# Cosine attention feeding a gated MLP on one core: k features, one difference and one weight sum on GpSimd, the last product in two PSUM banks, and a fixed table of step priorities

## The chip, the core and the metric

The kernel runs on one core of a Trainium2 chip. The metric is the device time of one execution in microseconds (us); lower is better. Before the change the median of three runs is 285.66 us (285.08 to 286.04).

## What is computed

The inputs are `q`, `k`, `v` of shape (8 batches, 8 heads, 576 tokens, 64), `w_in` (512 x 2048) and `w_out` (2048 x 512), all float32. The output is 4608 x 512 float32.

```python
def phi(x, c, s):                       # c, s: cosine and sine of the token's place
    r = np.maximum(x, 0.0)
    return np.concatenate([r * c, r * s], axis=-1)
q_p, k_p = phi(q, cos_w, sin_w), phi(k, cos_w, sin_w)
kv  = einsum('bhsf,bhsd->bhfd', k_p, v);  z = sum(k_p, axis=2)
num = einsum('bhsf,bhfd->bhsd', q_p, kv); den = einsum('bhsf,bhf->bhs', q_p, z) + 1e-06
x = (num / den) transposed to (4608, 512)
h = x @ w_in
out = (h * cos(h)) @ w_out
```

## The kernel before

The eight batches of attention feed nine chunks of 512 tokens of the two matrix products. A batch gives 512 tokens to the chunk of its own number, and its remaining 64 tokens go into a ninth chunk (`xR`). Chunk c has a first layer (`layer1`, output `gT`) and a second (`layer2` or `layer2_plain`, output staged in one of three tiles `ost` and stored from GpSimd's queue, line L803).

**Attention of a batch.** `load` (L394, L397) fetches q, k and v by SyncE's queue into `qm`, `km`, `vm`, one tile of each for all batches, so that the load of the next batch waits until the features of this one are made. `prep` makes features: ten instructions for k and ten for q per batch (five token groups, cosine and sine), each 128x512 float32 to float16 into `KQ`, as a Relu with a scale on ScalarE (L419) or as max and multiply on VectorE (L420). `cast_v` (L433, L434) makes float16 of v. `kv` (L446) multiplies k features by v in 40 matmuls of TensorE. `q_dma` (L485) transposes the q features by a DMA of SyncE's queue, `num` (L507, then L523 to L527) gives x, and `x_dma` (L557) or `x_pe` (L547) transposes x into `xT`.

**The products.** From chunk 1 the second layer, and from chunk 3 half of the first, is a Strassen-like product of seven in place of eight block products. It needs sums and differences of the operands, made by VectorE: of the weights once (`w_out_sums` L857 makes `T1` to `T4`, `w_in_sums` L676), of x in four instructions per chunk (`layer1_sums`, L697, tiles `XS0` to `XS3`), and of `gT` (L879, L924). The gate is a sine on ScalarE (L577) and a multiplication on VectorE (L579). Results leave PSUM by ScalarE copies (L748, L908) and VectorE additions (L752, L912). In the last chunk the last product (`a22` by `T4`) adds to bank `A`, whose two halves are then copied by ScalarE (L943) and VectorE (L945) and stored by two DMAs, one from SyncE's and one from ScalarE's queue.

**The order of the work.** Nothing is issued by the functions above directly. Each calls `Plan.add` with an engine (or a choice of engines), assumed costs, a due time and the data that it reads and writes. `Plan.run` then lays all steps out with a model of the engines, and each engine gets its instructions in the order of the modelled starts. A step may have a choice of VectorE and ScalarE (`either`); the plan takes one. In the model a step with `port=True` on VectorE and one with `port=True` on GpSimd exclude each other. The plan of before starts from the due times, passes forward and backward over the steps and tries 117 random changes of the priorities, keeping the best modelled end:

```python
        now = passes([s["due"] for s in self.steps], self.PASSES)
        for _ in range(self.ROUNDS):
            amp, wide = rnd.choice((0.5, 1, 2, 4)), rnd.choice((20, 40, 80, 300))
```

GpSimd has in before only memsets, a few tiny copies that hold back loads (L970, L980, L995, L1002), the loads of the weights (L976, L990) and the stores of the output (L803).

Of the kernel before, what the change touches and what calls it, by code (L numbers as in the profile page):

```python
# [15 lines left out]


class Plan:

    LINK = {"PE": 0.12, "ACT": 0.05, "DVE": 0.05, "POOL": 0.1, "SP": 0.0}

    PASSES, ROUNDS = 12, 117  # L30

# [10 lines left out]
    def add(self, eng, occ, lat, due, fn, rd=(), wr=(), dma=None, lane=None, late=0.0,  # L42
            lazy=None, port=False):

# [26 lines left out]
    def run(self):  # L73

        best = [math.inf]
        rnd = random.Random(1)

        def passes(key, n):
            local = None
            for _ in range(n):
                start, done = self.forward(key)
                end = max(done)
                if end < best[0]:
                    best[:] = [end, start, done, [s["eng"] for s in self.steps]]
                key = self.backward(start, done, end)
                if local is None or end < local[0]:
                    local = end, key  # L90
            return local
        now = passes([s["due"] for s in self.steps], self.PASSES)
        for _ in range(self.ROUNDS):
            amp, wide = rnd.choice((0.5, 1, 2, 4)), rnd.choice((20, 40, 80, 300))
            mid = rnd.uniform(0, best[0])
            key = [k + (rnd.gauss(0, amp) if abs(k - mid) < wide / 2 else 0) for k in now[1]]
            new = passes(key, 4)
            if new[0] < now[0] + 0.02:
                now = new
        for s, a, b, e in zip(self.steps, *best[1:]):  # L100
            s["start"], s["end"] = a, b
            s.update(zip(("eng", "occ", "lat", "fn"), s["opts"][e]))
        return sorted(self.steps, key=lambda s: (s["start"], s["n"]))

# [112 lines left out]

    def backward(self, start, done, end):
        st = self.steps
        left = [0] * len(st)  # L220
        for s in st:
            for d in s["deps"]:
                left[d] += 1
            if s["prev"] is not None:
                left[s["prev"]] += 1
        limit = [end - done[n] + start[n] for n in range(len(st))]
        late = [0.0] * len(st)
        free = {e: end for e in self.LINK}
        ready = {e: [] for e in self.LINK}
        for n, k in enumerate(left):  # L230
            if not k:
                ready[st[n]["eng"]].append(n)
        for _ in st:
            best = None
            for e, cand in ready.items():
                if not cand:
                    continue
                at = {n: min(free[e], limit[n] + st[n]["occ"]) for n in cand}
                top = max(at.values()) - self.PATIENCE.get(e, 0.0)
                k, t, n = max((start[n], at[n], n) for n in cand if at[n] >= top)  # L240
                if best is None or t > best[0]:
                    best = (t, e, n)
            t, e, n = best
            ready[e].remove(n)
            late[n] = free[e] = t - st[n]["occ"]
            for d in st[n]["deps"]:
                limit[d] = min(limit[d], late[n] - self.link(d, n) - (done[d] - start[d]))
                left[d] -= 1
                if not left[d]:
                    ready[st[d]["eng"]].append(d)  # L250
            d = st[n]["prev"]
            if d is not None:
                limit[d] = min(limit[d], late[n] - 0.01)
                left[d] -= 1
                if not left[d]:
                    ready[st[d]["eng"]].append(d)
        return late


@with_exitstack  # L260
def kernel(
# [24 lines left out]
    def blocks(ap, n):  # L286
        return ap.rearrange("(p f) ... -> f p ...", f=2)[n]
# [66 lines left out]
    Q_PE, X_PE = (), range(1, 3)  # L354
    VCAST = ("DVE", "ACT")
    LAZY = 8.0
    LATE_BY, LATE_W = (0.0, 1.0, 3.0, 1.0), 0.6
# [19 lines left out]
    def either(due, cost, fn, rd, wr):  # L377

        lat = {"DVE": 0.13, "ACT": 0.15, "POOL": 0.15}
        pl.add([(e, cost[e], cost[e] + lat[e], fn[e]) for e in cost], 0, 0, due, None, rd, wr, port=True)  # L380

# [28 lines left out]
    def prep(b, nm, t, g, eng, due, hs=slice(0, H), after=()):  # L410
        dst = (kp if nm == "k" else qp)
        out_, in_ = dst[:, t, hs, g, :], raw[nm][:, hs, t, :]
        sc = CS[:, b % 2, g, t:t + 1]
        heads = range(H)[hs]
        rd = hk(nm, heads) + ["CS", *after]
        wr = [(nm + "p", t, g, h) for h in heads]
        f = len(heads) / H
        cost = {"DVE": 0.09 + 0.33 * f, "ACT": 0.12 + 0.5 * f}
        fn = {"ACT": lambda: nc.scalar.activation(out=out_, in_=in_, func=AF.Relu, scale=sc),  # L419
              "DVE": lambda: nc.vector.tensor_scalar(  # L420
                  out=out_, in0=in_, scalar1=0.0, scalar2=sc, op0=ALU.max, op1=ALU.mult)}
        either(due, {e: c for e, c in cost.items() if eng in (e, "")}, fn, rd, wr)

# [265 lines left out]
    def layer1_sums(c, X, xk):  # L689
# [6 lines left out]
        def tt(n, a, b, rd, wr=()):  # L696
            dve(0.33, start[c] - 1 + 0.3 * n, lambda: nc.vector.tensor_tensor(  # L697
                out=XS[n], in0=a, in1=b, op=ALU.subtract), xk + rd, [("XS", i, n)] + list(wr), port=True)
        tt(0, b12, b11, [], (hk("k") + hk("q") + hk("v") + ["AL"]) if c == B - 1 else
# [105 lines left out]
    def store(c, h, o, due, fs=None):  # L805
        O = ost[o]
        keys = [("ost", o, f) for f in range(2)]
        if c < B:
            n = c % 2
            five, four = rows(c)  # L810
            put(due, five[:, 2 * h:2 * h + 2, :], blocks(O, n), keys, nc.gpsimd, "POOL")
            put(due, four[:, 2 * h:2 * h + 2, :], blocks(O, 1 - n), keys, nc.gpsimd, "POOL")
            return
        for n in range(2):
            f = slice(0, Dm) if fs is None else slice(fs * MH, (fs + 1) * MH)
            dst = out.rearrange("(i n s) m -> n i s m", n=2, s=S)[n][2 * h:2 * h + 2, 0:S5, f]
            put(due, dst.rearrange("i (p t) m -> p t i m", t=NT + 1)[:, NT], blocks(O, n)[:, :, f],
                keys if fs is None else [("ost", o, fs)],
                *((nc.scalar, "ACT") if n else (nc.sync, "SP")), nb=262.0 if fs is None else 131.0)

# [29 lines left out]
    def w_out_sums():  # L850
# [4 lines left out]

        def tt(out_, a, b, op, rd, wr):
            dve(1.14, start[2] - 8, lambda: nc.vector.tensor_tensor(  # L857
                out=out_, in0=a, in1=b, op=op), rd, wr, port=True)
        tt(T3, b22, b12, ALU.subtract, wk, ["T3"])
        tt(T1, b12, b11, ALU.subtract, wk, ["T1"] + wk[0:2])  # L860
# [3 lines left out]
    def layer2(c):  # L864
# [24 lines left out]

        def product(bank, a, b, rd, first, last):  # L890
            n = next(order)
            for tt in range(2):
                due = w0 + (n - 0.5 + 0.5 * tt) / 7 * ww * 0.97

                def mm(tt=tt):
                    for j in range(JH):
                        nc.tensor.matmul(  # L897
                            bank[0][:, tt * MH:(tt + 1) * MH], lhsT=a[:, j, tt * P:(tt + 1) * P],
                            rhs=b[:, j, :], start=(first and tt == 0 and j == 0),
                            stop=(last and tt == 1 and j == JH - 1), skip_group_check=True)  # L900
                pe(JH, MMH, due, mm, rd, [bank[1]])
            return due
# [33 lines left out]
        if c == B:  # L936
            store(c, 1, oh, d + 1.0, 1)
        d = product(A, a22, T4, gk(1, 1) + ["T4"], False, True)
        if c < B:
            copy(ost[oh][:, :, m0], A, [("ost", oh, 0)], d + 0.5)  # L940
            store(c, 1, oh, d + 1.5)
        else:
            act(0.3, d, lambda: nc.scalar.activation(  # L943
                out=ost[oh][:, 0, m0], in_=view(A)[:, 0], func=AF.Copy), [A[1]], [("ost", oh, 0)])
            dve(0.33, d, lambda: nc.vector.tensor_copy(  # L945
                out=ost[oh][:, 1, m0], in_=view(A)[:, 1]), [A[1]], [("ost", oh, 0)])
            store(c, 1, oh, d + 1.0, 0)


# [111 lines left out]
    def attention(b):  # L1061
# [3 lines left out]
        for t in range(NT + 1):  # L1065
            for g in range(2):
                prep(b, "k", t, g, "", T + 1.2 * t)
        for t, nt in ((0, 2), (2, 2), (4, 1)):
            cast_v(b, t, "", T + 6 + 0.4 * t, nt=nt)
        kv(b, T + 8)  # L1070
        for t in range(NT + 1):
            due = T + 8 + 1.2 * t
            for g in range(2):
                prep(b, "q", t, g, "", due)
            if b in Q_PE:
# [68 lines left out]
```

## Time and profile before

| | |
|---|---|
| median of 3 runs | 285.66 us (285.08 to 286.04) |
| profiled execution, span from first to last instruction | 282.8 us |
| the median less this span | 2.9 us; a device time of the profiled execution itself is not listed |
| TensorE busy, share of the span | 272.4 us, 96% |
| VectorE busy | 247.5 us, 88% |
| ScalarE busy | 215.5 us, 76% |
| GpSimd busy | 26.0 us, 9% |
| granted TensorE clock | 0.998 |
| k features: ScalarE L419, 56 of 128x512 | 38.3 us, 719 ns each |
| k features: VectorE L420, 24 of 128x512 | 10.7 us, 489 ns each |

A busy TensorE in this table is not TensorE at its peak, since ends of matmuls are modelled. VectorE and ScalarE instructions overlap by some 0.1 us at their ends, so that the busy time of a group is less than its count times its mean. "Idle before, releaser" in a group tells how long the engine stood idle just before such an instruction and what ended the wait.

### The profile page before, as it was taken

How to read it: one execution, taken by the hardware profiler on the slowest of the kernel's cores; microseconds unless marked ns; L12 is line 12 of the kernel's file. 1: busy time of each engine (PE TensorE's matmuls, PEld its weight loads, DVE VectorE, ACT ScalarE, POOL GpSimd, SP SyncE). 2: the span in 40 equal slices, each digit the busy share in tenths (PEclk: the TensorE clock that was granted, in tenths of full speed). 3: DMA queues.
4: the chain of work that ended last, by engine and by line, in shares of the span. 5: the costliest groups of instructions: out<-in, count | busy, mean ns of one | idle time of the engine just before them, and what ended most of it. 6: DMA issues, size and time to landing. Idle time of an engine off the chain costs nothing.

```text
span 282.8 us, 6578 instructions
## 1 busy us (share of the span) xinstructions
PE 272.4 (96%) x2619; PEld 208.3 (74%) x2619; DVE 247.5 (88%) x458; ACT 215.5 (76%) x367; POOL 26.0 (9%) x53
## 2 busy tenths in 40 slices
PE   7889989999999999999999999999999999999993
PEld 2468856669866688777877887787777877876882
DVE  2986878999999999999999999999899999967941
ACT  2947897999999999999999999995834666456420
POOL 1412020011000020002000200020002001100200
PEclk9999999999999999999999999999999999999999
DMA  6999999799989999999997899786024001100124
GB/s 214 303 204 273 258 310 300 251 270 212 344 222 240 228 227 362 170 245 224 254 268 186 265 290 224 164 159 167 2 56 168 21 2 75 76 2 0 68 82 150
DMA packets 77567, 53.30 MB, mean 188 GB/s; under 512 B 46048, under 2 KB 75232, under 8 KB 77536
## 3 DMA queue, kind: packets, MB, share of 16 engines
q1 hardware_dynamic: 70032, 39.73, 55.7%
q0 software_dynamic: 6784, 12.59, 17.1%
q10 hardware_dynamic: 720, 0.57, 0.6%
q8 instruction: 20, 0.33, 0.5%
q14 instruction: 11, 0.09, 0.1%
HBM read 36.74 MB, written 9.44 MB: 163 GB/s over the span
## 4 chain that ended last, share of the span: by engine, by line
PE 84%; DMA 8%; ACT 3%; DVE 2%; issue 1%; SPq 0%; ACTq 0%; DVEq 0%
PE M L897 33%; PE M L636 16%; PE M L740 8%; PE M L604 8%; PE TR L740 4%; PE M L834 4%; DMA vm<-in_v_dram 4%; PE TR L636 3%; PE ATT L507 3%; DMA qT<-KQ 3%; PE ATT L446 3%; DMA qm<-in_q_dram 2%; ACT KQ L419 1%; PE M L475 1%; DVE x L527 1%
## 5 line engine op out<-in xcount | busy, mean ns | idle before, releaser
L577 ACT ACTIVATE ch<-M 128x512 f32<-128x512 f32 x90 | 52.8, 595 | 11.1 <-PE M L604 4.1
L897 PEld LDWEIGHTS <-gT 128*128 128x128 f16 x560 | 53.7, 98 | 9.3
L579 DVE TENSOR_TENSOR gT<-M,ch 128x512 f16<-128x512 f32 x83 | 55.4, 683 | 4.7 <-ACT ch L577 4.2
L897 PE MATMUL M<-w_out_sb,gT 128*128 128x256 f16 x448 | 54.9, 273 | 0.0
L636 PE MATMUL M<-xT,w_in_sb 128*128 128x512 f16 x184 | 45.9, 379 | 0.0
L419 ACT ACTIVATE KQ<-qm,CS 128x512 f16<-128x512 f32 x59 | 40.1, 718 | 4.5 <-DMA qm<-in_q_dram 4.5
L419 ACT ACTIVATE KQ<-km,CS 128x512 f16<-128x512 f32 x56 | 38.3, 719 | 0.0
L636 PEld LDWEIGHTS <-w_in_sb 128*128 128x128 f16 x256 | 24.4, 98 | 18.3
L803 POOL DMA_DIRECT2D out_dram<-ost x32 | 17.0, 537 | 213.9 <-DVE ost L912 134.8
L897 PE MATMUL M<-T,S 128*128 128x256 f16 x256 | 32.5, 273 | 0.0
L604 PE MATMUL M<-xT,w_in_sb 128*128 128x256 f16 x256 | 30.6, 273 | 0.1
L897 PEld LDWEIGHTS <-S 128*128 128x128 f16 x256 | 24.9, 98 | 4.0
L604 PEld LDWEIGHTS <-w_in_sb 128*128 128x128 f16 x256 | 24.5, 98 | 3.9 <-issue 0.3
L908 ACT ACTIVATE ost<-M 128x512 f32<-128x512 f32 x31 | 18.5, 597 | 10.2 <-PE M L897 10.1
L527 DVE TENSOR_TENSOR x<-ATT,rec 128x512 f16<-128x512 f32 x32 | 22.1, 691 | 1.1
L740 PEld LDWEIGHTS <-w_in_sb 128*128 128x128 f16 x192 | 18.5, 98 | 4.9 <-issue 0.2
L912 DVE TENSOR_TENSOR ost<-M,ost 128x512 f32<-128x512 f32 x24 | 16.4, 681 | 4.0 <-issue 3.5
L507 PEld LDWEIGHTS <-qT 128*128 128x128 f16 x320 | 15.1, 98 | 4.7 <-issue 0.5
L752 DVE TENSOR_TENSOR Z<-M,Z 128x512 f32<-128x512 f32 x23 | 15.6, 684 | 2.3 <-PE M L740 1.9
L879 DVE TENSOR_TENSOR S<-gT 128x2048 f16<-128x2048 f16 (+1 forms) x16 | 17.3, 1085 | 0.2
L748 ACT ACTIVATE Z<-M 128x512 f32<-128x512 f32 x19 | 11.3, 596 | 6.6 <-PE M L740 6.4
L740 PEld LDWEIGHTS <-WS 128*128 128x128 f16 x144 | 13.6, 98 | 3.3 <-issue 0.2
(130 smaller groups left out, 421.8 us busy)
## 6 DMA issues: line engine op xcount, KB each, us to landing
out_dram<-ost POOLq DMA_DIRECT2D x32, 256.0 KB, 4.3
qm<-in_q_dram SPq DMA_DIRECT2D x8, 640.0 KB, 5.8
km<-in_k_dram SPq DMA_DIRECT2D x8, 640.0 KB, 7.8
qm<-in_q_dram SPq DMA_DIRECT2D x8, 512.0 KB, 5.6
km<-in_k_dram SPq DMA_DIRECT2D x8, 512.0 KB, 6.7
vm<-in_v_dram SPq DMA_DIRECT2D x6, 640.0 KB, 6.4
vm<-in_v_dram SPq DMA_DIRECT2D x6, 512.0 KB, 5.9
w_in_sb<-in_moe_w_in_dram POOLq DMA_DIRECT2D x4, 512.0 KB, 8.9
```

Source lines behind the costliest of these rows:

```text
L419: fn = {"ACT": lambda: nc.scalar.activation(out=out_, in_=in_, func=AF.Relu, scale=sc), "DVE": lambda: nc.vector.tensor_scalar(out=out_, i ...
L507: nc.tensor.matmul(bank[hb][:, hh * D1:(hh + 1) * D1], lhsT=a[:, h, :], rhs=z[:, h, :], start=(i == 0), stop=(i == len(parts) - 1))
L527: nc.vector.tensor_tensor(out=split(x16[n][:, hs, :], k), in0=A[:, :, :, 0:D], in1=split(rec[n][:, hs], k).unsqueeze(3).broadcast_to((P, k ...
L577: act(0.5, due, lambda: nc.scalar.activation(out=ch[c], in_=bank, func=AF.Sin, bias=math.pi / 2.0, scale=1.0), [key], [("ch", c)])
L579: mul(due, 0.61, lambda q: q.tensor_tensor(out=dst, in0=bank if len(dst.shape) == 2 else bank.rearrange("p (j s) -> p j s", j=dst.shape[1] ...
L604: nc.tensor.matmul(M1[m][:, jj * 2 * P:(jj + 1) * 2 * P], lhsT=w_in_sb[:, cc, j * P:(j + 1) * P], rhs=X[:, cc, ts], start=(cc == 0), stop= ...
L636: nc.tensor.matmul(M, lhsT=w_in_sb[:, cc, j * P:(j + 1) * P], rhs=X[:, cc, :], start=(cc == 0), stop=(cc == NCT - 1))
L740: nc.tensor.matmul(bank[0][:, j * TH:(j + 1) * TH], lhsT=a(cc, j), rhs=b[:, cc, :], start=(first and j == 0 and cc == 0), stop=(last and j ...
L803: pl.add(eng, 0.9 if eng == "POOL" else 0.65, 0, due, lambda: q.dma_start(out=dst, in_=src_), keys, [], dma=(nb, 355.0))
L879: dve(0.07 + 1.07 / NG, due, lambda: nc.vector.tensor_tensor(out=out_[:, sl], in0=a[:, sl], in1=b[:, sl], op=op), rd, wr, port=True)
L897: nc.tensor.matmul(bank[0][:, tt * MH:(tt + 1) * MH], lhsT=a[:, j, tt * P:(tt + 1) * P], rhs=b[:, j, :], start=(first and tt == 0 and j == 0),
L908: act(0.5, due, lambda: nc.scalar.activation(out=dst, in_=view(bank), func=AF.Copy), [bank[1]], dk)
```

## The change

From batch 2 on all ten k feature instructions of a batch have GpSimd as their only engine (60 instructions). `XS2`, one of the four differences of x, goes from VectorE to GpSimd in each of the six chunks that have it. The weight sum `T3` goes from VectorE to GpSimd. The last product of the last chunk no longer adds to bank `A`: bank `A` is copied to `ost` while that product runs into two other banks, one for each half; VectorE adds each half to `ost`, and each half is stored by two DMAs of half the size. The random search is gone: a table of 1319 numbers, one for each step in the order of `add`, gives the priorities, and the plan is one forward pass with them. GpSimd's steps do not have `port=True`.

The diff, cut to its core:

```diff
+KEYS = (
+    -85, 45, 175, 387, -79, -14, 51, 116, 181, 246, 311, 376, 1113, 1267, 1502, 1163, 1972, 2582,
...
+)
     def run(self):
-        best = [math.inf]
-        rnd = random.Random(1)
...
+        st = self.steps
+        assert len(KEYS) == len(st)
+        start, done = self.forward([k / 100 for k in KEYS])
+        for s, a, b in zip(st, start, done):
             s["start"], s["end"] = a, b
...
+    XPOOL = (2,)
+    KPOOL, QPOOL = (0, 1), ()
...
     def prep(b, nm, t, g, eng, due, hs=slice(0, H), after=()):
-        cost = {"DVE": 0.09 + 0.33 * f, "ACT": 0.12 + 0.5 * f}
+        cost = {"DVE": 0.09 + 0.33 * f, "ACT": 0.12 + 0.5 * f, "POOL": 0.15 + 0.75 * f}
+              "POOL": lambda: nc.gpsimd.tensor_scalar(
+                  out=out_, in0=in_, scalar1=0.0, scalar2=sc, op0=ALU.max, op1=ALU.mult),
...
     def layer1_sums(c, X, xk):
+            if n in XPOOL:
+                pl.add("POOL", 1.3, 1.45, due - 2, lambda: nc.gpsimd.tensor_tensor(
+                    out=XS[n], in0=a, in1=b, op=ALU.subtract), rd, wr)
...
     def w_out_sums():
+            if pool:
+                pl.add("POOL", 4.7, 4.9, start[2] - 8, lambda: nc.gpsimd.tensor_tensor(
+                    out=out_, in0=a, in1=b, op=op), rd, wr)
-        tt(T3, b22, b12, ALU.subtract, wk, ["T3"])
+        tt(T3, b22, b12, ALU.subtract, wk, ["T3"], True)
...
+    def store_tile(o, i, due):
+        for n in range(2):
+            dst = out.rearrange("(i n s) m -> n i s m", n=2, s=S)[n][2 + i, 0:S5, 0:MH]
+            put(due, dst.rearrange("(p t) m -> p t m", t=NT + 1)[:, NT], blocks(ost[o], n)[:, i, 0:MH],
+                [("ost", o, 0, i)], *((nc.scalar, "ACT") if n else (nc.sync, "SP")), nb=65.5)
...
     def layer2(c):
-            act(0.3, d, lambda: nc.scalar.activation(
-                out=ost[oh][:, 0, m0], in_=view(A)[:, 0], func=AF.Copy), [A[1]], [("ost", oh, 0)])
-            dve(0.33, d, lambda: nc.vector.tensor_copy(
-                out=ost[oh][:, 1, m0], in_=view(A)[:, 1]), [A[1]], [("ost", oh, 0)])
-            store(c, 1, oh, d + 1.0, 0)
+        copy(ost[oh][:, :, m0], A, [("ost", oh, 0, i) for i in range(2)], d + 0.5)
+        d = product(BANKS2, a22, T4, gk(1, 1) + ["T4"], True, True, True)
+        for i, (bank, key) in enumerate(BANKS2):
+            dst = ost[oh][:, i, m0]
+            dve(0.33, d, lambda dst=dst, bank=bank, i=i: nc.vector.tensor_tensor(
+                out=dst, in0=bank[:, i * MH:(i + 1) * MH], in1=dst, op=ALU.add), [key, ("ost", oh, 0, i)],
+                [("ost", oh, 0, i)])
+            store_tile(oh, i, d + 1.0)
...
     def attention(b):
-                prep(b, "k", t, g, "", T + 1.2 * t)
+                prep(b, "k", t, g, "POOL" if g in KPOOL else "", T + 1.2 * t)
```

In the built program GpSimd has 60 feature instructions, 6 differences and `T3` more, and one more instruction ahead of its first feature, which loads a library of GpSimd's. The features of batch 2 and `T3` stand between the loads of `w_out` and the stores of chunk 0. The features that stay with a choice are split anew: q features on VectorE are 24 in place of 21, on ScalarE 56 in place of 59; k features of the first two batches are 11 on VectorE and 9 on ScalarE. TensorE has as many instructions of each kind as before, in another order, with few differences in the first 40 us.

## The prediction

> **What bounds the kernel now.** I read the share of the engines first, then the busy time by stage, then what TensorE waits for, then the end.
>
> The page's engine line says nothing yet of a bound:
>
> ```profile
> PE 272.4 (96%) x2619; PEld 208.3 (74%) x2619; DVE 247.5 (88%) x458; ACT 215.5 (76%) x367; POOL 26.0 (9%) x53
> ```
>
> By stage (span, then PE, PEld, DVE, ACT, POOL busy us, clock, DMA share, GB/s), all three engines are nearly full from 60 to 200 us, and after that TensorE and VectorE:
>
> ```profile
> 60.00:200.00 140.00, 139.76 (x1428) 109.26 (x1426) 134.60 (x239) 131.49 (x224) 9.52 (x18) 1.00 0.95 233
> 200.00:278.00 78.00, 77.93 (x657) 60.94 (x654) 65.42 (x109) 39.29 (x67) 6.34 (x12) 1.00 0.16 53
> ```
>
> TensorE stands still for 0.24 and 0.07 us there. Busy ends are modelled, so I check the starts: in the chain of waits eight 128x256 matmuls follow each other in 0.87 us (109 ns each), four 128x512 in 0.86 (216 ns). Its waits are few, and asked for 60 to 278 us alone the same view lists none:
>
> ```profile
> PE M L475 <- ACT KQ L419: 1.6, 1, 1.6
> PE ATT L965 <- POOL S L951: 1.3, 1, 1.3
> PE M L834 <- DMA w_out_sb<-in_moe_w_out_dram: 0.7, 1, 0.7
> PE ATT L507 <- DVE kvz L460: 0.4, 1, 0.4
> PE TR L547 <- DVE x L527: 0.3, 1, 0.3
> PE M L475 <- DVE qT L481: 0.2, 1, 0.2
> PE ATT L446 <- ACT V L433: 0.2, 1, 0.2
> ```
>
> So TensorE is the bound, at full clock, and the other two just keep up with it. The change takes no matmul away. It can gain only what is idle: these waits and the end. It can lose much more.
>
> **The feature work that leaves.** Start to start, a feature costs 0.396 us on VectorE and 0.613 on ScalarE (the rows' 0.48 and 0.72 overlap the next one), a difference 0.335, `T3` 1.13. Off VectorE go 13 k features (5.1), six differences (2.0) and `T3` (1.1), and three q features come (1.2): 7.0 us less. Off ScalarE go 47 k and three q features: 50 x 0.613 = 30.7 us less. For the time this is worth 0: TensorE waits for neither from 60 us on. It is slack, 0.31 us of idle time at most turned into gain; I take 0.2.
>
> **What GpSimd pays.** No row shows an elementwise GpSimd instruction of full size. Nearest is its memset of 128x512 float16, 0.524 us, which only writes. A feature that reads while it writes costs at least that, 0.52; one pass after the other 1.05. I take 0.9, near the upper end, since its input is twice as wide and it does two operations. `T3` is four times as long with two inputs: between 2.1 (four memsets) and 6.3 (three passes); I take the middle, 4.2. A difference is 0.52 to 1.57, middle 1.05. The Trainium skill, "GPSIMD Engine Reference", section "Elementwise — side-by-side cycle accounting", speaks against the whole move (elementwise work is slower there than on VectorE) and gives 769 ns for 512 elements in its best loop and 4497 ns for a two-input 2048; by these the chain below would be 12.2 us in place of 13.2.
>
> Per batch that is 10 x 0.9 + 1.05 + four store issues of 0.54 = 12.2 us of some 26.5: no throughput bound. The place that counts is batch 2. In the built order GpSimd makes two features, `T3`, then eight features, and only then the kv matmuls of batch 2 may run. The k load lands at 37.43 + 12.3 = 49.7 us (issue and longest time to landing in the view of tile km), the last `w_out` piece at 36.70 + 12.7 = 49.4. GpSimd is then free: in before it did nothing from 37.5 to 57.55, which also covers the library load ahead of the first feature (unseen in the trace, 0 to 12 us without cost). 49.7 + 10 x 0.9 + 4.2 = 62.9. TensorE reaches these 40 matmuls at about 64.4: in before the second half starts at 64.05, and by the counts of matmuls ahead the new order has 0.3 us more in front. Cover 1.5 us; bounds 57.0 (7.4 early) and 66.5 (2.1 late).
>
> **The shared port.** Now the waits that are new. GpSimd beside VectorE features looks like this (start, us, engine):
>
> ```profile
> 23.76 0.19 POOL L980 COPY w_out_sb<-w_in_sb 1x4 f16<-1x4 f16 x1 [6.16 <-DMA w_in_sb<-in_moe_w_in_dram]
> 35.14 0.53 POOL L1002 CAST w_out_sb<-qm 1x2 f16<-1x2 f32 x1 [9.24 <-DMA qm<-in_q_dram]
> 34.35 1.27 DVE L420 TENSOR_SCALAR KQ<-km,CS 128x512 f16<-128x512 f32 x3
> ```
>
> Two copies of a few elements: 0.19 us alone, 0.53 when VectorE's features run until 35.62. So 0.34 us per GpSimd instruction that meets them. In return L420 took 611 ns at most, where the median is 478: 0.13 us. From 49.7 to 64.4 VectorE has, in the new order, five q features, two casts of v, `T1` and `T2`: 5 x 0.396 + 0.34 + 0.60 + 2 x 1.13 = 5.2 us, 35% of the stretch. 11 instructions x 0.34 x 0.35 = 1.3: the chain ends at 64.2, 0.2 before TensorE asks. That costs 0, barely.
>
> The Trainium skill, "SBUF — State Buffer", section "Who interferes with whom", says that the later of the two waits until the first has finished, also where VectorE only reads two SBUF inputs. The copy above agrees; for two-input instructions no row here shows it. Taken whole, the rule would add all of VectorE's 5.2 us to GpSimd's chain and end it 3.7 us late.
>
> **Moved steps and their queues.** The stores of chunk 0 now stand behind batch 2's features on GpSimd (57.55 before, 62.9 or later now); chunk 1's second tile of results needs `ost0` only in its second layer, which starts at 68.6 and writes it late: 0. Chunk 1's stores stand behind batches 3 and 4; chunk 1 stored at 101.93 before, and batch 4's features end about ten us after batch 3's kv, which has 77.3 us of matmuls ahead of it and so stands near 87, with the 10 us of idle time until then: 0. SyncE's k load of batch 3 must wait for GpSimd (62.9, in before 55.95), but the order now has the four q transposes ahead of it; landing in 5.3 us and ten features give 77 to 78 against a kv at 87, cover 9 us. `T3` is read near 90 by the same count. `XS2` is read by the fifth product of its group, four products of 0.43 later, cover 1.7 against 1.05; uncovered it costs 0.7 a chunk.
>
> **The start.** Of the seven waits the first two (first load, memset) stay. The other five, 1.8 us, may move with the order: two qT copies now stand behind the casts of v, which wait for their load, and the second `w_out` load is issued behind a 0.18 us copy. Bounds +0.9 and -1.8; I take -0.3, near nothing, since the loads are the same.
>
> **The end.** Before:
>
> ```profile
> 277.96 0.38 ACT L943 ACTIVATE ost<-M 128x256 f32<-128x256 f32 x1 [4.77 <-PE M L897]
> 278.38 0.42 DVE L945 COPY ost<-M 128x256 f32<-128x256 f32 x1 [1.60 <-ACT ost L943]
> 278.84 0.64 ACTq L803 DMA_DIRECT2D out_dram<-ost  x1
> ```
>
> One bank, so the two copies follow each other. In two banks half 0 is added under half 1's matmuls, and half 1's addition (0.42, as the 128x256 additions from PSUM) ends 0.45 after the last matmul in place of 0.88: 0.43 less. Against it: three DMA issues of 0.64 or more now follow each other on ScalarE's queue, and the last may start as late as before. For it: the last DMAs are half as long. Bounds 0 and -0.8; I take -0.5.
>
> **Sum.** -0.2 - 0.3 - 0.5 = -1.0. On the profiled span that is 282.8 to 281.8; the median of the runs lies 2.9 above that span, so 285.66 becomes 284.7. The forecast's own range is 283.4 to 286.0.
>
> **Rivals.** First, GpSimd is late for batch 2's kv (slower). Place: 64.4 us, TensorE in order with nothing to put ahead. It decides as soon as a feature with its waits costs over about 1.05 us (14.7 us to land, less 4.2, over ten). At 1.05 and 6.3 plus 1.3 of waits the chain ends at 67.8, 3.4 late; with VectorE's 5.2 us shut out it is 3.7 late. TensorE never makes that up: +3.5 - 1.0 gives 288.2. For it: the copy of 0.53 us and a cover of 0.2. Against it: the memset's 0.52 leaves room.
>
> Second, VectorE becomes the bound between 60 and 200 us: it has 5.4 us free there and wins 7. Some 80 of its instructions there use the port; if each waits half a feature (0.45) in the 37% of the time in which GpSimd works, that is 13.3 of these 12.4. Whole features would give 26.6, so 0 to +14, taken as +4; less 1.0 that is 288.7. Against it: the 0.13 of the row, 80 x 0.13 = 10.
>
> Third, more is gained: all 1.8 us of the start's waits and the end's 0.43: 283.1. For it, freer engines at 40 to 60 us; against it, loads that do not move.
>
> **Chances.** The forecast 0.55, late GpSimd 0.25, VectorE the bound 0.08, the larger gain 0.12. A measurement here tells 0.3%, 0.86 us. The forecast's sum lies on that edge: 0.30 faster, 0.25 same. With 0.12 from the larger gain and 0.01 from a small lateness: faster 0.42, same 0.26, slower 0.32. The range 283.0 to 289.0 takes in the late cases and most of the larger gain.
>
> **What would show it.** Right: no wait of TensorE from 60 to 278 us; features of 0.8 to 1.0 us on GpSimd; kv of batch 2 waiting for no one near 64; the last store issued 0.4 us after the last addition's old place or earlier. Wrong: a wait of TensorE's L446 for GpSimd's `KQ`; VectorE features or gate sums much over 0.48 and 0.68 us; a TensorE busy share under 99% in the middle.

## The result and the profile after

| | before | after |
|---|---|---|
| median | 285.65 us (4 runs) | 344.25 us (339.51 to 346.32, 4 runs) |
| profiled execution: span, time | 282.8 us, not listed | 337.4 us, 339.51 us |
| granted clock of it | 0.998 | 0.939 |

The kernel became much slower: the ratio is 1.195, with a 95% interval of 1.190 to 1.200. Two of the four runs were slower at a lower clock still and are left out of the ratio; the other two have a median of 341.4 us, 55.8 us above before, and the losses and gains below are counted from there. The prediction was 284.7 us in a range of 283.0 to 289.0.

The page of the changed kernel, its engine line and GpSimd's first group:

```profile
PE 284.4 (84%) x2619; PEld 215.4 (64%) x2619; DVE 253.2 (75%) x442; ACT 188.5 (56%) x317; POOL 164.9 (49%) x120
...
L444 POOL TENSOR_SCALAR KQ<-km,CS 128x512 f16<-128x512 f32 x60 | 126.3, 2118 | 34.3 <-DMA km<-in_k_dram 19.8
```

A feature took 2118 ns on GpSimd, where the prediction had taken 900. TensorE's share fell from 96% to 84%. The span is 54.6 us longer. Of these TensorE was idle for 42.6 (337.4 - 284.4 = 53.0, before 282.8 - 272.4 = 10.4) and busy for 12.0 more with the same 2619 matmuls. By stage (span, then PE, PEld, DVE, ACT, POOL busy us, clock, DMA share, GB/s), the changed kernel:

```profile
60.00:200.00 140.00, 113.34 (x1071) 86.20 (x1069) 108.70 (x181) 82.21 (x138) 96.74 (x58) 0.93 0.82 190
200.00:278.00 78.00, 61.48 (x572) 48.10 (x570) 53.71 (x89) 36.80 (x63) 42.59 (x30) 0.87 0.42 108
```

These are the two stretches of time in which TensorE stood still for 0.24 and 0.07 us before (the work in them is not quite the same, since the changed kernel is behind). Now no engine is full: TensorE has 81%, VectorE 78%, GpSimd 69% from 60 to 200 us. That is the picture of engines that wait for each other in turn, not of an engine that is the bound. The view of waits names them for TensorE (us in total, times, longest):

```profile
PE ATT L472 <- POOL KQ L444: 25.3, 7, 8.2
PE M L772 <- POOL XS L726: 12.7, 2, 10.2
PE M L630 <- DVE gT L605: 3.7, 2, 2.4
```

The first is the one that the prediction gave as the sign of its first rival (then L446, now L472). The first two sum to 38.0 us, beside the 42.6 us of idle time that came in. GpSimd's timeline over batch 2 shows the chain that the prediction had summed (start, us, count at the end of the name), and over batch 6 where `XS2` stands:

```profile
49.88 3.98 POOL L444 TENSOR_SCALAR KQ<-km,CS 128x512 f16<-128x512 f32 x2 [12.84 <-DMA km<-in_k_dram]
53.84 4.05 POOL L898 TENSOR_TENSOR T<-w_out_sb 128x2048 f16<-128x2048 f16 x1
57.89 16.68 POOL L444 TENSOR_SCALAR KQ<-km,CS 128x512 f16<-128x512 f32 x8
...
190.52 19.94 POOL L444 TENSOR_SCALAR KQ<-km,CS 128x512 f16<-128x512 f32 x9
210.43 1.15 POOL L726 TENSOR_TENSOR XS<-xT 128x512 f16<-128x512 f16 x1
```

TensorE's timeline at the ends of these two chains (the wait and its releaser in brackets):

```profile
74.63 2.33 PE L472 MATMUL ATT<-V,KQ 128*128 128x65 f16 x39 [7.16 <-POOL KQ L444]
...
211.62 1.01 PE L772 MATMUL M<-XS,WS 128*128 128x256 f16 x4 [10.16 <-POOL XS L726]
```

The features of batch 2 begin at 49.88, where the prediction had 49.7, and end at 74.57, where it had 62.9 to 64.2. TensorE had nothing else to do from 67.47 on, 7.16 us before its next matmul. At 210.43 the 1.15 us of `XS2` come after nine features: TensorE's product waited 10.16 us for it.

The last two additions and stores of the changed kernel, which answer to the copies and the store shown of before:

```profile
332.94 0.82 DVE L993 TENSOR_TENSOR ost<-M,ost 128x256 f32<-128x256 f32 x2 [0.66 <-ACT ost L954]
333.39 1.42 ACTq L835 DMA_DIRECT2D out_dram<-ost  x2
```

The last matmul ends at 333.29 and the span at 337.36, 4.07 us later; before these were 277.93 and 282.78, 4.85 us. So the end gained 0.8 us.

### The profile page after: what moved, and what is told of

Read it like the earlier page. It is cut to its first block, busy times and chain, and to the rows that moved or that the text cites. A ratio compares the mean times of both kernels' runs of the same rounds, so it can differ in the third digit from the quotient of the medians.

```text
span 337.4 us, 6606 instructions
## 1 busy us (share of the span) xinstructions
PE 284.4 (84%) x2619; PEld 215.4 (64%) x2619; DVE 253.2 (75%) x442; ACT 188.5 (56%) x317; POOL 164.9 (49%) x120
## 3 DMA queue, kind: packets, MB, share of 16 engines
q1 hardware_dynamic: 70048, 39.73, 48.2%
## 5 line engine op out<-in xcount | busy, mean ns | idle before, releaser
L444 POOL TENSOR_SCALAR KQ<-km,CS 128x512 f16<-128x512 f32 x60 | 126.3, 2118 | 34.3 <-DMA km<-in_k_dram 19.8
L835 POOL DMA_DIRECT2D out_dram<-ost x32 | 17.9, 562 | 84.9 <-DVE ost L958 52.7
L662 PE MATMUL M<-xT,w_in_sb 128*128 128x512 f16 x184 | 47.3, 391 | 0.0
L443 ACT ACTIVATE KQ<-qm,CS 128x512 f16<-128x512 f32 x56 | 37.7, 713 | 4.3 <-DMA qm<-in_q_dram 4.3
L662 PEld LDWEIGHTS <-w_in_sb 128*128 128x128 f16 x256 | 25.1, 100 | 20.7 <-issue 2.0
L472 PE MATMUL ATT<-V,KQ 128*128 128x65 f16 x280 | 15.1, 220 | 25.3 <-POOL KQ L444 25.3
L630 PE MATMUL M<-xT,w_in_sb 128*128 128x256 f16 x256 | 31.8, 278 | 4.3 <-DVE gT L605 3.7
L943 PE MATMUL M<-T,S 128*128 128x256 f16 x256 | 33.5, 277 | 0.0
L472 PEld LDWEIGHTS <-KQ 128*128 128x128 f16 x320 | 15.1, 114 | 28.5 <-POOL KQ L444 26.2
L630 PEld LDWEIGHTS <-w_in_sb 128*128 128x128 f16 x256 | 25.0, 100 | 8.7 <-issue 4.9
L489 ACT ACTIVATE kvz<-ATT 128x520 f16<-128x520 f32 x7 | 4.2, 605 | 33.5 <-PE ATT L472 33.4
L772 PEld LDWEIGHTS <-w_in_sb 128*128 128x128 f16 x192 | 18.7, 100 | 5.7 <-issue 1.1
```

The costliest lines, as they stand in the source:

```text
L444: "POOL": lambda: nc.gpsimd.tensor_scalar(out=out_, in0=in_, scalar1=0.0, scalar2=sc, op0=ALU.max, op1=ALU.mult),
L472: nc.tensor.matmul(bank[hb][:, hh * D1:(hh + 1) * D1], lhsT=kp[:, t, h].rearrange("p g d -> p (g d)"), rhs=V1[:, t, h, :], start=(t == 0), ...
L630: nc.tensor.matmul(M1[m][:, jj * 2 * P:(jj + 1) * 2 * P], lhsT=w_in_sb[:, cc, j * P:(j + 1) * P], rhs=X[:, cc, ts], start=(cc == 0), stop= ...
L662: nc.tensor.matmul(M, lhsT=w_in_sb[:, cc, j * P:(j + 1) * P], rhs=X[:, cc, :], start=(cc == 0), stop=(cc == NCT - 1))
L772: nc.tensor.matmul(bank[0][:, j * TH:(j + 1) * TH], lhsT=a(cc, j), rhs=b[:, cc, :], start=(first and j == 0 and cc == 0), stop=(last and j ...
L835: pl.add(eng, 0.9 if eng == "POOL" else 0.65, 0, due, lambda: q.dma_start(out=dst, in_=src_), keys, [], dma=(nb, 355.0))
```

## The experiments

The theory after the result was that the price of a feature on GpSimd is the step that failed. The rivals were the port that VectorE and GpSimd share, and the order that the table of priorities fixes.

**The features go back.** `XS2`, `T3`, the table and the new end stay.

```diff
-    KPOOL, QPOOL = (0, 1), ()
+    KPOOL, QPOOL = (), ()
```

> The k features of batches 2 to 7 go back to the plan's choice of VectorE and ScalarE; XS2, T3, the table of priorities and the new end stay. Theory (a GpSimd feature costs 1.98 us by itself where 0.9 was assumed, and ten of them in series hold up kv): nearly the whole loss goes, 284 to 289 us. Rival 1 (the shared port is what costs, and T3 and XS2 on GpSimd hold VectorE too: T3 held one q feature for 3.0 us): 288 to 295. Rival 2 (the order from the table is bad by itself): over 300.

Measured: 293.26 us, ratio 1.027 (1.024 to 1.030). Of the 55.8 us lost, 48.2 come back with the features. But 7.7 stay, more than the theory had: the time lies in the range of the port rival. That rival cannot be the whole cause, since most of the loss is gone; what the 7.7 us are is asked by the next run and three later ones.

**The features alone.** `XS2` and `T3` go back to VectorE, the features stay on GpSimd.

```diff
-    XPOOL = (2,)
+    XPOOL = ()
-        tt(T3, b22, b12, ALU.subtract, wk, ["T3"], True)
+        tt(T3, b22, b12, ALU.subtract, wk, ["T3"])
```

> Only the k features stay on GpSimd; XS2 and T3 return to VectorE. Theory: the loss stays but for T3's 4.05 us in the chain of batch 2 and two waits for XS2 (12.7 us in the list of waits): 325 to 340 us. Rival 1 (port): more returns, since T3 blocked VectorE longest: 310 to 325. Rival 2 (table): no change, 339 to 345.

Measured: 341.39 us, ratio 1.197 (1.189 to 1.204), as the whole change. The theory's 325 to 340 was missed, and the time lies where the table rival had it; but the table with the new end alone takes 287.55 us (below), so the table is not what makes the loss. The 12.7 us of waiting for `XS2` are gone, and the waits for `KQ` are 36.8 us in place of 25.3: the lateness is that of GpSimd's queue, and whoever asks next pays it. So the two losses that the view of waits lists apart do not add up to two gains.

**The price by itself.** A kernel that computes nothing of the reference, with GpSimd instructions one after the other.

```python
g.tensor_scalar(out=o(i), in0=in_, scalar1=0.0, scalar2=sc[:, 0:1], op0=ALU.max, op1=ALU.mult)  # as the kernel
g.tensor_scalar(out=o(i), in0=in_, scalar1=0.0, scalar2=None, op0=ALU.max)                      # one operation
g.tensor_copy(out=o(i), in_=in_)                                                               # a cast
```

> Computes nothing of the reference: GpSimd instructions by themselves, six of each form with VectorE at rest, then eight features beside VectorE features, beside two-input VectorE differences, and beside VectorE products from PSUM. Theory: the feature as the kernel has it costs 1.98 us with VectorE at rest, and what costs is the second operation or the scalar read per partition: one operation alone 0.8 to 1.2, a cast 0.5 to 0.8; strides, float32 and the output's type change it by under 0.2; about 0.1 us are fixed, so 128x256 costs 1.0. Beside VectorE features or two-input instructions it is 0.1 to 1.2 longer, beside products from PSUM not. Rival 1 (port): under 1.0 at rest and 2.0 only beside VectorE.

Its groups (busy us, mean ns of one), in order: the kernel's form, one operation, 256 columns, the difference's form, 128 columns, the cast:

```profile
L56 POOL TENSOR_SCALAR kq<-km,sc 128x512 f16<-128x512 f32 x6 | 11.9, 1998 | 9.1 <-DMA km<-in_k_dram 9.1
...
L60 POOL TENSOR_SCALAR kq<-km 128x512 f16<-128x512 f32 x6 | 8.8, 1503 | 0.0
L71 POOL TENSOR_SCALAR kq<-km,sc 128x256 f16<-128x256 f32 x6 | 6.8, 1205 | 0.0
L73 POOL TENSOR_TENSOR o<-flat 128x512 f16<-128x512 f16 x6 | 6.1, 1108 | 0.0
L71 POOL TENSOR_SCALAR kq<-km,sc 128x128 f16<-128x128 f32 x6 | 4.2, 773 | 0.0
L62 POOL CAST kq<-km 128x512 f16<-128x512 f32 x6 | 3.4, 637 | 0.0
```

Start to start the feature takes 1.973 us with VectorE at rest, one operation 1.450, the cast 0.552; 256 columns take 1.120 and 128 take 0.693. Without strides, with a float32 output and with a float16 input it is the same within 0.003 us. So what is dear in this form of instruction is its arithmetic: the first operation adds 0.90 us to the cast (the expectation had 0.8 to 1.2 for the whole instruction), the second 0.52, or 0.43 with both scalars as constants (1.885 us). The number of operations alone does not give the price, though: the difference, one operation on two float16 inputs, takes 0.998. Then eight features ran beside VectorE instructions: features as GpSimd's, differences of 2048 columns with two inputs in SBUF, and products with one input in PSUM (start, us for all eight):

```profile
100.78 17.51 POOL L80 TENSOR_SCALAR kq<-km,sc 128x512 f16<-128x512 f32 x8
...
119.76 23.24 POOL L80 TENSOR_SCALAR kq<-km,sc 128x512 f16<-128x512 f32 x8
...
143.54 15.81 POOL L80 TENSOR_SCALAR kq<-km,sc 128x512 f16<-128x512 f32 x8
```

Beside the products a feature costs what it costs alone (15.81 / 8 = 1.98). Beside VectorE's features it is 2.19 on average, with VectorE done after half of the stretch. Beside the differences it is 2.9, and the differences take 1.26 and 1.63 us in turn, where in before such an instruction takes 1.13 start to start. The port is real, but in the kernel it adds only some 0.12 us to a feature (mean 2.118 against 1.998 here); the price makes 1.10 of the 1.22 us by which the prediction was short.

**Half as wide.** Each GpSimd feature computes heads 0 to 3 alone.

```diff
-                  out=out_, in0=in_, scalar1=0.0, scalar2=sc, op0=ALU.max, op1=ALU.mult),
+                  out=out_[:, 0:HB], in0=in_[:, 0:HB], scalar1=0.0, scalar2=sc, op0=ALU.max, op1=ALU.mult),
```

> As the changed kernel, but each GpSimd feature covers heads 0 to 3 alone (128x256); the k features of heads 4 to 7 of batches 2 to 7 are left out. Number, order and queues of the instructions stay. Theory: a feature costs about 1.0 us, the prediction's 0.9 within 0.1, and then the rest of the prediction should hold: 284 to 290 us, kv of batch 2 waiting under 2 us. Rival 1 (port): there are as many meetings with VectorE, so at least half of the loss stays: 300 to 315. Rival 2 (table): over 320.

Measured: 299.47 us, ratio 1.045 (1.039 to 1.052); 1306 ns a feature in the kernel, waits for `KQ` 1.6 us. The theory's 284 to 290 was missed, with its price of 1.0 (1.12 by itself); that at least half of the loss stays, as the port rival had it, is false as well, since a quarter stays. The chain of batch 2 ended at 67.36, and TensorE had stood waiting from 66.24. By the prediction's rule, which turns at 1.05 us a feature, this had to be late, and it is by 1.2 us. The rest of the 14 us was not traced; `XS2` makes 3.6 us of TensorE's waits.

**Half as many.** Only the sine features of k go to GpSimd, at full width.

```diff
-    KPOOL, QPOOL = (0, 1), ()
+    KPOOL, QPOOL = (1,), ()
```

> The change as it is, but only five of the ten k features of a batch (the sine ones) on GpSimd; the other five are back on ScalarE and VectorE. GpSimd then has 5 x 2.1 + 1.2 + 2.2 = 13.9 us of the 26.5 of a batch, about what the prediction had reckoned for ten at 0.9 (12.2). Theory: the lateness goes nearly whole, since per batch there is room, and the time is that of the features-back run plus little: 291 to 300, with waits for KQ under 6 us in all. Rival (the late start and the port decide, not the sum per batch): 305 to 325.

Measured: 299.12 us, ratio 1.046 (1.040 to 1.052), waits for `KQ` 3.2 us. Half the work in either way gives the same time, with 30 instructions here and 60 there. That fits GpSimd's total (66.5 us busy with features here, 77.6 there) and not the number of instructions that meet on the port. It does not show it, since the two runs differ in VectorE's and ScalarE's work too: here the other five features are made there, in the half-width run half of each is made nowhere.

**A quarter as wide.** As half as wide, with heads 0 and 1 alone.

```diff
-                  out=out_, in0=in_, scalar1=0.0, scalar2=sc, op0=ALU.max, op1=ALU.mult),
+                  out=out_[:, 0:HB // 2], in0=in_[:, 0:HB // 2], scalar1=0.0, scalar2=sc, op0=ALU.max, op1=ALU.mult),
```

> The change as it is, but every GpSimd feature computes only heads 0 and 1 of its eight (128 columns instead of 512; heads 2 to 7 of the k features are left out from batch 2 on). By itself such an instruction takes 0.69 us, below the 0.9 that the prediction took. Full width (1.98) gave 344, half width (1.12) 299.5. Theory A, the price was the failed term and the rest of the sum holds: with 0.69 TensorE waits nowhere for KQ, and what stays over the table alone (287.55) is T3's and XS2's hold on VectorE: 289 to 294. Rival B, the number of meetings on the port counts and not the price: 60 instructions more make 295 to 300. Rival C, the prediction as it stood: 283.4 to 286.0.

Measured: 286.77 us, ratio 1.005 (1.003 to 1.007). This run is the prediction's own case, since a feature now costs in the kernel what the prediction took. Its group, and GpSimd's and TensorE's timelines at batch 2:

```profile
L444 POOL TENSOR_SCALAR KQ<-km,CS 128x128 f16<-128x128 f32 x60 | 52.6, 888 | 43.0 <-DMA km<-in_k_dram 22.2
...
51.09 4.07 POOL L898 TENSOR_TENSOR T<-w_out_sb 128x2048 f16<-128x2048 f16 x1
55.15 7.58 POOL L444 TENSOR_SCALAR KQ<-km,CS 128x128 f16<-128x128 f32 x8
...
65.36 0.83 PE L472 MATMUL ATT<-V,KQ 128*128 128x65 f16 x22
```

888 ns with the port's waits, the chain done at 62.73 (predicted 62.9 to 64.2), kv of batch 2 at 65.36 (predicted 64.4), and no wait of TensorE for GpSimd's `KQ` in the whole run. The time lies inside the prediction's range and 2.1 us over its forecast. It lies in none of the three ranges on record before the run: under theory A, which added the hold of `T3` and `XS2` to the table's time, and over the prediction's own. Every instruction keeps its place, and only the width of GpSimd's features, and so their price, differs: 341.4 became 286.77 us, 54.6 of the 55.8.

**What is left: the table, `T3`, `XS2`.** Three runs without any feature on GpSimd: neither `T3` nor `XS2` there, `T3` alone, `XS2` alone (the edits of the first two experiments, combined).

> GpSimd gets no elementwise work at all: the features, XS2 and T3 are back on ScalarE and VectorE; what is left of the change is the table of priorities and the last product in two banks. It settles where the 7.7 us come from that stayed when only the features went back (293.3 us against 285.5). Theory A, the port: T3 and XS2 on GpSimd held two-input VectorE instructions (VectorE was lengthened by 8.2 us in that run), so without them the time is 284 to 286.5, and no VectorE instruction over 3 us is left. Theory B, the table: its priorities were made for another division of the work, so that the order itself costs the 7.7 us; then 290 to 294, with the same waits of TensorE for gT, S and Z. Both in halves: 287 to 290.

> Table and new end as in the change; of the work on GpSimd T3 alone stays (one instruction of 4.05 us), features and XS2 are back. With neither T3 nor XS2 there the time was 287.55 us, with both 293.3. Theory A, the early hold: T3 holds a VectorE feature of batch 2 for 3.3 us at 50 us, and in an order that is fixed nothing makes it up, so 289.5 to 291.5. Rival B, the hold is hidden, since VectorE has slack there: 287 to 288.5, and XS2 is the costly one.

> Table and new end; of the work on GpSimd the six XS2 stay (1.2 us each), features and T3 are back. Theory A: XS2's six meetings with two-input VectorE instructions lengthened those by 4.2 us in the run with both, in the stage where TensorE and VectorE are both full, so about half of the 5.7 us between that run and the table alone is theirs: 289.5 to 291.5. Rival B: XS2 itself is fast and early enough, and T3 carries the loss: 287 to 288.5.

Measured: 287.55 us, ratio 1.007 (1.004 to 1.009), with neither; 289.61, 1.015 (1.012 to 1.017), with `T3`; 289.89, 1.015 (1.013 to 1.017), with `XS2`; and 293.26 with both. So the table's order with the new end costs 1.7 us, `T3` 2.1 more, the six `XS2` 2.3, and both together somewhat more than their sum. The first lies where both theories in halves had it (287 to 290), the other two where theory A had them. What `T3` and `XS2` do to VectorE is seen in the timelines. In the run with `T3` alone:

```profile
50.41 3.73 DVE L446 TENSOR_SCALAR KQ<-km,CS 128x512 f16<-128x512 f32 x2
...
49.40 4.06 POOL L898 TENSOR_TENSOR T<-w_out_sb 128x2048 f16<-128x2048 f16 x1 [12.53 <-DMA w_out_sb<-in_moe_w_out_dram]
```

Two VectorE features that take 0.48 us each last 3.73: the first started inside `T3` and ended 0.28 us after it. In the run with `XS2` alone a gate product with two inputs in SBUF (median 1.22 us) is lengthened beside a difference:

```profile
232.23 2.10 DVE L801 TENSOR_TENSOR gT<-Z,ch 128x1024 f16<-128x1024 f32 x1
...
231.91 1.35 POOL L726 TENSOR_TENSOR XS<-xR 128x512 f16<-128x512 f16 x1 [10.92 <-DMA xR<-x]
```

VectorE's instructions over their medians (counting those over by 0.1 us and more) sum to 3.5 us in the first run and 3.7 in the second, 7.5 in the run with both and 0.7 in the run with neither. In none of these runs is a wait of TensorE for GpSimd's `XS2` listed. So the hold on VectorE is the likely cause; by which wait it comes to TensorE was not followed.

**The end alone.** The kernel before, with its search, and the last product in two banks with four smaller stores.

```diff
-        d = product(A, a22, T4, gk(1, 1) + ["T4"], False, True)
+        copy(ost[oh][:, :, m0], A, [("ost", oh, 0, i) for i in range(2)], d + 0.5)
+        d = product(BANKS2, a22, T4, gk(1, 1) + ["T4"], True, True, True)
```

> The kernel before with one part of the change: the last product in two banks and its results stored in four half-size DMAs. Search, features, differences and T3 are as before. Theory (the step on the end in the prediction): 0.3 to 0.8 us less, that is 284.7 to 285.3 if before gives 285.5; the last store is issued 0.4 to 0.8 us sooner after the last matmul. Rival: the search draws another order for the rest, since it has other steps, and the middle moves by more than the end, up or down by 1 us.

Measured: 285.34 us against 285.84, ratio 0.999 (0.996 to 1.002). From the last matmul to the end it is 4.18 us (279.42 to 283.60) where before had 4.85, so the 0.7 us are there in the trace; the comparison of times cannot tell them from nothing. The rival has a part in it: the search drew another order, and the last matmul of this trace ends 1.5 us later than in before (277.93).

**Could a better order carry the change?** The random search of before lays out the changed kernel, with measured costs of GpSimd's steps: as it is, then with that order kept and the features a quarter as wide, then with a plan that also excludes GpSimd's steps from VectorE's marked ones. And with `T3` and `XS2` on GpSimd but no features. The second pair of lines is the third run's against the first; the difference and `T3` get `port=True` there too.

```diff
-        cost = {"DVE": 0.09 + 0.33 * f, "ACT": 0.12 + 0.5 * f, "POOL": 0.15 + 0.75 * f}
+        cost = {"DVE": 0.09 + 0.33 * f, "ACT": 0.12 + 0.5 * f, "POOL": 0.15 + 1.85 * f}
...
-    pl.add([(e, cost[e], cost[e] + lat[e], fn[e]) for e in cost], 0, 0, due, None, rd, wr, port="POOL" not in cost)
+    pl.add([(e, cost[e], cost[e] + lat[e], fn[e]) for e in cost], 0, 0, due, None, rd, wr, port=True)
```

> All of the change on GpSimd stays, but the order is planned anew by the random search of before, with the measured prices of GpSimd's instructions (2.0 us a feature where the change assumes 0.9, 1.15 a difference, 4.05 for T3). It asks whether the order or the division of work is at fault. Theory A, division: ten features, a difference and four store issues are 10 x 2.1 + 1.2 + 2.2 = 24.4 us of the 26.5 us of a batch, so a plan that knows it can hide most of it but not the start of the GpSimd chain and not the port: 295 to 320, the waits for KQ down to under 20 us in all. Rival B, wrong order: with true prices the plan hides everything, 286 to 290. Rival C: nothing helps, 335 to 345.

> The order planned for the measured prices (the run of 322.2 us), with the GpSimd features computing heads 0 and 1 alone, 0.69 us each (heads 2 to 7 of the k features are left out from batch 2 on). No instruction changes its place on its engine. Theory A, the division of work: the 36 us that this order loses at full width are GpSimd's price and what VectorE's two-input instructions lose beside it, so the time falls to 286 to 292. Rival B, the order itself: kv and the second layers stand in poor places because the plan waited for GpSimd, and the time stays at 300 or more.

> As the run of 322.2 us, planned with the measured prices, and now the plan also counts that GpSimd's elementwise steps and VectorE's marked ones exclude each other, which the change does not count. Theory A, the division: 60 x 2.0 us of GpSimd and some 90 us of marked VectorE instructions want the same port in the 185 us from 50 to 235, so whoever waits, the time stays well over 300: 305 to 325. Rival B, a plan that knows the port finds the room: 287 to 297.

> T3 and XS2 on GpSimd and the new end, no features there, and the order planned by the random search of before with measured prices in place of the table. It asks whether the 7.7 us of the run with features back can be had back by the order. Theory A, mostly the order: 285 to 288, since seven instructions of 10 us in all are little against 285. Rival B, the port's hold costs wherever the seven stand, since VectorE is 88% busy and the plan's model lets GpSimd's steps run beside VectorE's: 290 to 294.

Measured: 322.2 us, ratio 1.130 (1.125 to 1.135); 317.59, 1.112 (1.104 to 1.119); 338.61, 1.183 (1.173 to 1.193); 291.84, 1.020 (1.016 to 1.024). In the first run, with the measured prices, TensorE's waits for GpSimd's `KQ` fall to 0.5 us, and others take their place. The first two lines of its waits:

```profile
PE M L921 <- DVE S L901: 10.4, 5, 3.4
PE ATT L511 <- DVE x L531: 4.1, 6, 1.2
```

I had read this as the division of work, and expected the time to fall to 286 to 292 once the price is gone. It fell by 4.6 us only. In that run the features of batch 2 end at 63.30, and the kv matmuls stand where the plan had put them for a dear chain:

```profile
53.65 9.65 POOL L422 TENSOR_SCALAR KQ<-km,CS 128x128 f16<-128x128 f32 x10
...
78.09 1.07 PE L450 MATMUL ATT<-V,KQ 128*128 128x65 f16 x23 [1.64 <-DVE V L438]
```

So most of the 36 us stay with the order that this search found for dear features (`T3` and `XS2` on GpSimd are among them). A plan that knew of the port was worse still, outside both ranges expected for it; and without the features the search came to 291.84, where the port rival had it, no clear gain over the table's 293.26. Whether some other order carries ten full-width features a batch stays open. That these searches, with as many tries as before, found none is all that was shown.

## Why the prediction was wrong

**The price of a feature is the failed step.** "I take 0.9, near the upper end" with 0.52 to 1.05 as bounds: it is 1.98 by itself and 2.118 in the kernel, about twice the upper bound. The bounds were made from a memset, that is from an instruction that does no arithmetic, with one pass more for the reading. The runs show what this left out: a cast, which reads and writes, is at 0.552 beside the memset's 0.524, but each of the two operations of the feature adds 0.5 to 0.9 us (1.450 with one, 1.973 with two). By its own rule the prediction would then have had 49.7 + 10 x 2.0 + 4.2 = 73.9 for the chain of batch 2, 9.5 us after TensorE's arrival; measured 74.57. The Trainium skill, "GPSIMD Engine Reference", section "Elementwise — side-by-side cycle accounting", was the second support of the small number; its 769 ns for 512 elements, stated for its best loop, is matched by no two-operation instruction here (1.885 to 1.976 us), and the measurement decides.

**"No throughput bound."** 12.2 us per batch out of 26.5 become 10 x 2.1 + 1.2 + 2.2 = 24.4. The prediction looked at batch 2 as the one place that counts. With 24.4 of 26.5 there is little cover anywhere, and the load of k takes what is left: k has one tile, and its next load is issued when the features are made. The features of batch 2 end at 74.57, the load of batch 3 is issued from 74.60, its features start at 86.49 and end at 107.39: 32.8 us for a turn, where the prediction counted 26.5 for a batch. So kv waited for `KQ` seven times, in batches 2, 3, 5 and 7, and in batch 6 the product waited for `XS2`, which stood behind the features.

**The first rival had the mechanism and not the size.** The wait, its place and the point from which it decides (1.05 us with waits) were right: 0.888 gives no wait, 1.306 gives 1.2 us at batch 2. "TensorE never makes that up: +3.5" was the price of one late batch; four were late, batch 2 alone by over 7 us, and batch 6 by way of `XS2`.

**The `XS2` step.** "Cover 1.7 against 1.05." It takes 1.18 as a rule (1.05 taken), but it was reckoned from the moment its operands are there, and not from the moment GpSimd comes to it. Nine features stood ahead. `T3` was right: 4.05 for 4.2.

**The load of batch 3.** The prediction had it landed near 68 and the features done at 77 to 78, 9 us ahead of kv. At the quarter width, where the chain of batch 2 is as predicted, the features of batch 3 run from 75.73 to 86.14 and kv starts at 86.78: the second of k's two loads is issued at 66.6, behind the transposes and the two loads of q, and takes up to 9.0 us. Cover 0.6 in place of 9; the dear features hid this error.

**The shared port.** 1.3 us of GpSimd's waits in batch 2 and 0.13 us per VectorE instruction were a fair total. The chain of batch 2 took 24.69 us where ten features and `T3` by themselves make 23.8, so 0.9 us were waits. VectorE's instructions over their medians sum to 9.9 us in the changed kernel (0.8 in before), the prediction's 80 x 0.13 = 10. But they are 15 instructions, beside four between 11 and 15 us of a kind that is long in before as well, and not 80: features, casts of v and instructions with two inputs in SBUF, the longest a feature of 3.50 us that started inside `T3`. The rule of the Trainium skill, "SBUF — State Buffer", section "Who interferes with whom", which the prediction gave as a bound, agrees with the runs: the later one waits until the first has finished (`T3` above), and the products that read PSUM do not meet GpSimd at all (1.98 us). The second rival, VectorE as the bound, is false at 78% busy; but the 5.7 us between the table alone and the table with `T3` and `XS2` are most likely this port (VectorE's lengthening grows from 0.7 to 7.5 us), and the prediction's sum charged nothing for it where VectorE is nearly full.

**Freed work "worth 0".** Against before that holds. But at the quarter width, with `T3` and `XS2` on GpSimd, the kernel took 286.77, and with the features back on VectorE and ScalarE 293.26. So VectorE's freed time did pay for what `T3` and `XS2` held up, or else the table, which was made for this division, fits the other badly; these two were not told apart.

**The order of the table.** The prediction gave the start -0.3 and the middle -0.2. The table alone took 1.7 us more with an end that is 0.7 better, so its order costs 2.4. In the trace of that run (its slowest, 288.62 us) TensorE is idle for 2.45 us from 60 to 200 us where before had 0.24, and for 7.11 us before 60 where before had 5.26.

**The end.** -0.5 between 0 and -0.8: measured -0.8 in the changed kernel and -0.7 alone.

**A slip in the third rival.** Its two terms give 285.66 - 1.8 - 0.43 = 283.4 and not 283.1. Nothing in the outcome rests on it.

## What to carry to other kernels

A price for an instruction that the trace does not show must be bounded by rows of the same form of instruction with the same arithmetic; a memset bounds only the writing, and where no such row is there the range has to hold a factor, not a half. When ten instructions per batch go to an idle engine, ask what share of its time they fill at twice their price: everything that stands in that queue behind them, a small difference or a store, becomes late with them, and so does the next load where it waits for the same tile. Work that a plan puts on GpSimd should be planned with its measured price and its hold on VectorE's two-input instructions, and an order found for one division of the work is not the order for another.

## What the runs showed of the hardware

- On GpSimd the price goes by the form of the instruction: 128x512 takes 0.552 us as a cast, 0.998 as a difference of two float16 inputs, 1.450 as `tensor_scalar` with one operation and 1.973 with two. The last costs about 0.26 us and 3.34 ns per column, a line through 0.473, 0.693, 1.120 and 1.973 us at 64, 128, 256 and 512 columns.
- Beside one GpSimd instruction of 4.06 us a VectorE feature of 0.48 us lasted 3.78 us (3784 ns, in the run with the features back).
- After a long wait TensorE's matmuls ran at half their rate: after the 10.16 us wait for `XS2` the 128x256 matmuls followed each other every 0.213 us (212.006, 212.220, 212.433), where in before it is 0.109, and the granted clock from 211.60 to 213.20 us was 0.50. The Trainium skill, "TensorE: Matmul & The Clock Gate", section "Part 1: The HAM clock gate (the "warmup" mystery)", states a halved clock after an idle window of about 3.4 us. The halved clock agrees; the length of the window was not tested here. So a long wait costs more than itself: with such waits TensorE was busy for 12.0 us more with the same matmuls.
